# The same steps of an attention and gated feed-forward kernel in another hand-written order

## The chip, the core and the metric

The kernel runs on one core of one Trainium2 chip. A core has a matrix engine (TensorE, here PE, with its weight loads shown as PEld), a vector engine (DVE), a scalar engine (ACT), GpSimd (POOL) and a synchronization engine (SP). Each takes its own instructions in the order in which they are written, and waits for the others through semaphores. The time is that of one execution on the device in microseconds (us), a median over runs. TensorE writes into a small memory of eight banks, called bank 0 to 7 here; one bank holds 512 fp32 columns of 128 partitions.

## The reference

Eight batches, eight heads, 576 positions, head width 64. Linear attention without a softmax, a root-mean-square norm per head, then a gated feed-forward layer whose gate is a convolution over three positions:

```python
kv  = einsum('bhsd,bhse->bhde', k, v)
out = einsum('bhsd,bhde->bhse', q, kv)
rms = sqrt(mean(out * out, axis=-1, keepdims=True) + 1e-06)
x   = (out / rms * g_norm)              # heads side by side: (8, 576, 512)
h   = maximum(x @ w_in, 0.0)            # (8, 576, 1024)
conv_out = sum(conv_w[k] * hp[:, k:k + S, :] for k in range(3))   # hp: h padded by one row
gate = 1.0 / (1.0 + exp(-conv_out))
result = h * gate @ w_out               # (8, 576, 512)
```

## The kernel before

The whole program is a list of 697 short steps in one string, ORDER. A loop at the end takes one token after another and issues its instructions; then every instruction is tied to the one before it on its engine, so that each engine's order is exactly the string's. What stands between tokens of different engines plays no part: only the order on each engine, the data that a step reads, and the buffers that it reuses.

A token is a name with numbers, then an optional choice after a colon (which of ACT and DVE does a copy or a relu) and slots after an @ (which bank, or which buffer of a ring). `hm.2.4@0` is x @ w_in for batch 2 and the fifth of eight column blocks of 128, into banks 0 and 1. A step that writes into a bank waits until the steps that read the former contents are done. The choice differs by step: with `:1` a relu (re) goes to DVE, without it to ACT; kvn, ky, kvc, oc, ea and eh are the same; ca, qc0 and qc go to ACT with `:1` and to DVE without; dg goes to DVE with `:1`.

The steps, in the order in which a batch goes through them (line numbers are those of the kernel before):

- Loads, all from POOL's queue: `pre` (batch 0, in pieces of two heads, L245, and two more pieces from SP), Lq, Lk, Lv (one batch each, L304; batch 1 in two halves, `.0` and `.2`), Li.0 to Li.3 (w_in by quarters of its columns, L318; Li.1 holds column blocks 2 and 3), Lo.0 and Lo.1 (w_out by halves, L325). A load of a batch waits until its ring buffer (two for each of q, k and v) is free.
- kv: k^T v on PE (L361). Batches 0 and 1 copy it into a block-diagonal weight (kvc), the others into kvn, and with the halves of the partitions exchanged into kvx (ky, by an engine; kx, by SP's queue).
- q transposed: on PE (qt0, qt at L383; qtp at L391) and copied out (qc0, qc), or by SP's queue (dq, L439) for batches 5, 6 and 7.
- q (kv): ot on PE for batches 0 and 1 (L433, L434), oq for the others (L467), by tiles of two heads.
- The norm. Batches 0 and 1: sq (square, ACT, L494 or L496), on (sum over a head on PE), nl (reciprocal root, ACT, L545), mu0 (scale, DVE, L565); the last tile of batch 0 in halves: sqh (L517), onh (L523), nlh (L531), muh (L538). The others: sq and oc (square and plain copy, L496 and L344), ss (sums of all tiles on PE, L578), ln (root, L587), sl (split in two bf16 parts, DVE, L594 to L597), sp (spread over partitions on PE, L606), mu (L632); or fw, fr by way of memory for batches 6 and 7 (mu at L628). The root and the sigmoid of ACT need different tables; a table load (L217) is issued where ACT's order goes from one to the other, 12 times.
- hm: x @ w_in (L643), eight matmuls of 288 columns; ha and hb (L658, L666) are the same in two parts. re: the relu (L649 on ACT, L651 on DVE).
- The gate: ta (two taps, DVE, L702 and L703), aa and ab (adds, L709 and L715), sg (sigmoid, ACT, L748), mg (product, DVE, L754). Two column blocks of batch 0 take the three taps on PE instead (dg makes diagonal weights, L722; cm, L734; sg at L745).
- om: the product with w_out (L764) by tiles of 128 rows; for the first and last pair of batches in two parts (`.0` and `.4`); oh for the last tile (L781). ea, eh evict (L344 on ACT, L346 on DVE), st, sh store from SP's queue.
- `unread.n.i` issues n matmuls of ones that nobody reads (L430), 26 in all. pi, ps, pn, pg, pc, pl and ct make small constants: ct transposes the convolution's weights on PE, pc works out their ratios on DVE in six small instructions, ps and pl make the matrices that sp and ss use (pl by memsets on POOL).

The last lines of the program, which make the string the engines' order:

```python
    prev = {}
    for ins in list(nc.cur_bb.bb.instructions):
        e = ins.engine
        if e in prev:
            tc.add_manual_dep(
                ins, prev[e].name,
```

Of the kernel before, what the change touches and what calls it, by code (L numbers as in the profile page):

```python
# [850 lines left out]
```

## Time and profile before

| | |
|---|---|
| time, median of 3 runs | 176.29 us (176.2 to 176.9) |
| span of the profiled execution | 174.7 us |
| instructions profiled | 3978 |
| from HBM, to HBM | 34.88 MB, 9.73 MB |

The profiled execution has a span from its first to its last instruction of 174.7 us; the runs' times include 1.6 us more than that (176.29 - 174.7). A row of the timeline reads: start and length in us, engine, line, operation, what is written from what, how many were merged, and in brackets the idle time of the engine before it and what ended it. In the groups, the busy time and the mean length in ns stand behind the bar, then the idle time before. "q_sb" is the buffer of q, "bank" the matrix engine's banks, "xT" the normalized x, "h" the relu's result, "taps" the gate's buffers. "SPq" is SP's queue. For a DMA the time to landing runs from the start of its issue.

### The profile page before, as it was taken

What the parts mean: (1) busy time and instruction counts of PE and PEld (TensorE: products, weight loads), DVE (VectorE), ACT (ScalarE), POOL (GpSimd) and SP (SyncE); (2) the same over time, 40 slices, a digit from 0 to 9 for tenths busy, and PEclk for the clock granted to TensorE, in tenths of its full rate; (3) what the DMA queues carried; (4) which work ended last, traced back from release to release, by engine and by line L of the source; (5) the groups of instructions that cost most, each with busy time, mean ns of one, the idle gap of its engine ahead of it and who ended that gap; (6) DMA issues with size and microseconds to landing.
All of it is one profiled execution on the core that took longest, in us unless ns stands there. A gap on an engine that the chain in (4) does not pass through costs nothing.

```text
span 174.7 us, 3978 instructions
## 1 busy us (share of the span) xinstructions
PE 164.6 (94%) x1590; PEld 100.1 (57%) x1607; DVE 151.8 (87%) x248; ACT 144.0 (82%) x224; POOL 30.8 (18%) x54
## 2 busy tenths in 40 slices
PE   6988997899799999999999999999999999999992
PEld 2545765685644687744677774545687654444451
DVE  4166799999999999999999999999989999998520
ACT  4578897999999999999999998999988629766132
POOL 7994705313130001810000000000000000000000
PEclk9999999999999999999999999999999999999999
DMA  5999999999999999999999390477694400076285
GB/s 151 182 186 198 200 202 203 205 204 204 208 203 205 203 204 164 162 196 191 190 203 234 72 261 6 149 188 181 173 268 161 152 0 4 23 277 235 90 322 196
DMA packets 37450, 30.81 MB, mean 176 GB/s; under 512 B 8608, under 2 KB 32952, under 8 KB 37432
## 3 DMA queue, kind: packets, MB, share of 16 engines
q0 software_dynamic: 21760, 15.96, 60.7%
q1 hardware_dynamic: 15632, 14.59, 29.6%
q8 instruction: 12, 0.20, 0.4%
q14 instruction: 6, 0.05, 0.1%
q10 hardware_dynamic: 40, 0.01, 0.0%
HBM read 34.88 MB, written 9.73 MB: 255 GB/s over the span
## 4 chain that ended last, share of the span: by engine, by line
PE 76%; DVE 9%; DMA 4%; POOL 4%; ACT 2%; issue 2%; POOLq 0%; ACTq 0%
PE bank L764 35%; PE bank L643 30%; DMA w_in_sb<-in_moe_w_in_dram 4%; PE bank L361 3%; PE bank L467 2%; DVE taps L703 1%; DVE qT L346 1%; POOL q_sb L245 1%; DVE taps L709 1%; DVE h L754 1%; PE bank L606 1%; DVE taps L702 1%; POOL v_sb L245 1%; POOL k_sb L245 1%; PE bank L781 1%
## 5 line engine op out<-in xcount | busy, mean ns | idle before, releaser
L643 PE MATMUL bank<-xT,w_in_sb 128*128 128x288 bf16 x480 | 63.6, 286 | 0.3 <-ACT root L545 0.2
L764 PE MATMUL bank<-w_out_sb,h 128*128 128x512 bf16 x267 | 62.4, 379 | 0.8 <-issue 0.3
L643 PEld LDWEIGHTS <-w_in_sb 128*128 128x128 bf16 x480 | 46.0, 98 | 14.9 <-issue 1.6
L748 ACT ACTIVATE taps<-taps,cwn 128x1152 bf16<-128x1152 bf16 (+1 forms) x38 | 39.7, 1078 | 7.4 <-DVE taps L715 7.3
L764 PEld LDWEIGHTS <-h 128*128 128x128 bf16 x280 | 26.4, 98 | 31.0 <-issue 1.2
L649 ACT ACTIVATE h<-bank 128x576 bf16<-128x576 f32 x48 | 30.2, 656 | 3.0 <-PE bank L643 2.8
L344 ACT ACTIVATE row<-bank 128x512 f32<-128x512 f32 (+1 forms) x29 | 16.3, 595 | 8.8 <-PE bank L764 6.0
L754 DVE TENSOR_TENSOR h<-h,taps 128x2304 bf16<-128x2304 bf16 (+1 forms) x20 | 22.0, 1109 | 0.6 <-ACT taps L748 0.6
L709 DVE TENSOR_TENSOR taps<-taps 128x2304 bf16<-128x2304 bf16 (+1 forms) x19 | 21.5, 1134 | 0.2
L715 DVE TENSOR_TENSOR taps<-taps,h 128x2304 bf16<-128x2304 bf16 (+1 forms) x19 | 21.5, 1131 | 0.2
L496 ACT ACTIVATE sq<-bank 128x576 bf16<-128x576 f32 x28 | 17.8, 663 | 0.6 <-PE bank L467 0.3
L703 DVE TENSOR_SCALAR taps<-h,cwn 128x1152 bf16<-128x1152 bf16 (+1 forms) x38 | 17.8, 467 | 0.0
L702 DVE TENSOR_SCALAR taps<-h,cwn 128x1152 bf16<-128x1152 bf16 (+1 forms) x38 | 17.4, 457 | 0.3 <-ACT h L649 0.2
L217 ACT ACT_TABLE_LOAD x12 | 15.4, 1283 | 2.6 <-issue 2.4
L651 DVE TENSOR_SCALAR h<-bank 128x576 bf16<-128x576 f32 x16 | 11.8, 752 | 1.7 <-PE bank L643 0.8
L344 ACT ACTIVATE o<-bank 128x576 f32<-128x576 f32 x19 | 12.8, 674 | 0.0
L632 DVE SCALAR_TENSOR_TENSOR xT<-o,cw,bank 128x576 bf16<-128x576 f32 x16 | 12.2, 808 | 0.1
L304 POOL DMA_DIRECT2D q_sb<-in_q_dram x8 | 6.2, 770 | 30.2 <-PE bank L391 29.4
L430 PE MATMUL bank<-fill 128*128 128x512 bf16 x25 | 9.0, 481 | 1.5 <-DVE fill L232 1.5
L346 DVE COPY row<-bank 128x512 f32<-128x512 f32 (+1 forms) x8 | 5.4, 672 | 4.4 <-PE bank L781 2.4
L361 PE MATMUL bank<-v_sb,k_sb 96*64 96x64 bf16 x384 | 8.3, 197 | 0.7 <-ACT sq L496 0.5
L361 PEld LDWEIGHTS <-k_sb 96*64 96x64 bf16 x384 | 7.1, 112 | 2.9 <-issue 2.2
(94 smaller groups left out, 148.8 us busy)
## 6 DMA issues: line engine op xcount, KB each, us to landing
out_dram<-row SPq DMA_DIRECT2D x35, 256.0 KB, 2.6
q_sb<-in_q_dram POOLq DMA_DIRECT2D x6, 576.0 KB, 15.2
v_sb<-in_v_dram POOLq DMA_DIRECT2D x6, 576.0 KB, 14.6
k_sb<-in_k_dram POOLq DMA_DIRECT2D x6, 576.0 KB, 16.6
factor<-factor SPq DMA_DIRECT2D x8, 288.0 KB, 5.4
w_in_sb<-in_moe_w_in_dram POOLq DMA_DIRECT2D x4, 256.0 KB, 9.0
w_out_sb<-in_moe_w_out_dram POOLq DMA_DIRECT2D x2, 512.0 KB, 18.3
q_sb<-in_q_dram POOLq DMA_DIRECT2D x4, 144.0 KB, 4.7
```

Source lines behind the costliest of these rows:

```text
L344: nc.scalar.activation(to, fr, AX.Copy)
L361: nc.tensor.matmul(ps[i][i * D:(i + 1) * D, t - t0, :], k_sb[:, 2 * t + i, r * D:(r + 1) * D], v_sb[:, 2 * t + i, r * D:(r + 1) * D], star ...
L496: nc.scalar.activation(in_order(b, s), product(b, t), AX.Square)
L643: nc.tensor.matmul(ps[:, e, :HS], w_in_sb[:, t, f * P:(f + 1) * P], x[:, t, e * HS:(e + 1) * HS], start=(t == 0), stop=(t == NT - 1))
L649: nc.scalar.activation(to, fr, AX.Relu)
L702: nc.vector.tensor_scalar_mul(tap[:, 0, f % 2, :n, 8:8 + S], h[:, f], cwn[:, 0, f:f + 1])
L703: nc.vector.tensor_scalar_mul(tap[:, 1, f % 2, :n, :S], h[:, f], cwn[:, 2, f:f + 1])
L709: nc.vector.tensor_add(tap[:, 1, :, :n, :S], tap[:, 0, :, :n, 7:7 + S], tap[:, 1, :, :n, 1:1 + S])
L715: nc.vector.tensor_add(y, y, h[:, 2 * j:2 * j + 2])
L748: nc.scalar.activation(y, y, AX.Sigmoid, scale=cwn[:, 1, f:f + 1])
L754: nc.vector.tensor_mul(h, h, T["tap", c, j][:, 1, :, :n, :S])
L764: nc.tensor.matmul(T["om", p, m], h[:, f, m * P:(m + 1) * P], w_out_sb[:, f, :], start=(f == 0), stop=(f == NF - 1))
```

## The change

The string is replaced by another one. It has the same 697 steps with the same sizes; their order differs on all engines and in POOL's queue of loads, and so do the banks and ring buffers, and for 56 steps the choice between ACT and DVE. The beginning, before and after:

```diff
-pre@0,0,0 Lq.1.0@1 unread.10.0@1 qt0.0.0@0 qt0.0.1@1 ca.k.0:1 pi ca.v.0:1 qc0.0.0:1@0 unread.2.2@2
-kv.0.0.1@3 pn kv.0.1.1@2 kvc.0.0.1.0:1@0 kvc.0.0.1.1 kvc.0.1.1.1 qc0.0.1 unread.3.4@0 kvc.0.1.1.0 ot.0.1@4 ct@1
-unread.1.3@0 sq.0.1@0 pg Li.1 unread.2.1@2 on.0.1@0 ot.0.0@6 qt0.0.2@2 pc Li.3 nl.0.1@0 Lk.1.0@1 sq.0.0@0 al.x0@0
...
-Lq.1.2 ot.0.3@2 sqh.0.3.0@0 mu0.0.2 qt.1.0@0 sqh.0.3.1 onh.0.3.0@6 qc.1.0@0 onh.0.3.1 nlh.0.3.0@1 nlh.0.3.1 ha.0.2@4
-muh.0.3.1 ha.0.3@0 muh.0.3.0 ps dg.6 Lv.1.2 hm.0.6@6 dg.7 hb.0.2 re.0.2:1 hm.0.7@2 hb.0.3 re.0.6 cm.0.6@4 sg.0.6@0
+pre@0,0,0 Li.1 Lq.1.0@1 Li.3 al.x0@0 ca.k.0 Lk.1.0@1 unread.2.2@5 Lv.1.0@1 unread.10.0@0 ca.v.0 kv.0.0.1@5
+kvc.0.0.1.0@0 Li.0 Lk.1.2 al.h1@1 ps pi ct@7 pn qt0.0.1@0 pg dg.7:1 qt0.0.0@2 qc0.0.0:1@0 qc0.0.1 kv.0.1.1@7
...
+unread.2.1@3 ot.0.3@4 mu0.0.2 qt.1.0@2 qc.1.0@0 Lq.2.0@0 sqh.0.3.0@4 sqh.0.3.1 onh.0.3.0@0 onh.0.3.1 nlh.0.3.0@7
+muh.0.3.0 nlh.0.3.1 ha.0.2@6 ha.0.3@2 muh.0.3.1 hm.0.6@0 hb.0.2 pc hm.0.7@4 hb.0.3 Lv.2.0@0 al.h0@0 re.0.2:1 ta.0.2@0
```

Batch 1's norm, and the stretch up to the sums of batches 2 and 3:

```diff
-re.0.0:1 unread.3.1@0 ta.0.0@2 sq.1.0@0 on.1.0@2 nl.1.0@0 hm.0.1@0 ot.1.1@6 qt.1.1@2 re.0.1 ab.0.1 kv.1.2.2@0 mu0.1.0
-sq.1.1@0 kvc.1.2.2.1 on.1.1@4 qc.1.1@0 kvc.1.2.2.0 ot.1.3@2 mg.0.3 Li.2 ta.0.1 ot.1.2@0 nl.1.1@0 mu0.1.1 hm.0.4@4
...
-oq.2.3@0 Lk.3.0@1 aa.1.1 Lq.3.0@1 kv.3.0.4@4 ta.1.1 sq.2.2@2 sq.2.3@3 ss.2@5 kvn.3.0.4:1 re.1.4 oc.2.2:1@1 qtp.3.0@2
-Lo.0 oc.2.3 ky.3.0.4.1 ky.3.0.4.0 ln.8@0 qtp.3.1@0 qc.3.0@0 qc.3.1@1 oq.3.1@6 oq.3.0@2 ab.1.3 oq.3.2@0 sq.3.0@0
-oc.3.0@2 aa.1.0 sq.3.1@1 sl.8@0 om.0.1.0@4 Lo.1 oc.3.1 al.x2@0 ab.1.1 sq.3.2@2 om.0.3.0@5 om.0.2.0@2 Lq.4.0@0 oq.3.3@6
+ot.1.0@0 hm.0.0@2 re.0.0:1 hm.0.1@4 re.0.1:1 ta.0.0@2 sq.1.0@4 on.1.0@6 nl.1.0@4 mu0.1.0 ta.0.1 qt.1.1@2 qc.1.1:1@2
+ot.1.1@4 sq.1.1@4 unread.1.1@6 kv.1.2.2@7 kvc.1.2.2.1 Lk.3.0@1 kvc.1.2.2.0:1 Lv.3.0@1 aa.0.0 ab.0.0 on.1.1@0 nl.1.1@5
...
+kvn.3.0.4 hm.1.5@2 unread.3.1@7 oc.2.2@2 oc.2.3 qtp.3.0@0 re.1.5 ky.3.0.4.1:1 ss.2@4 ln.8@0 Lk.5.0@1 qtp.3.1@5
+Lq.5.0@1 qc.3.0@1 oq.3.0@0 sq.3.0@0 oq.3.1@2 sq.3.1@2 om.0.2.0@7 aa.1.0 om.0.3.0@4 oc.3.0@1 oc.3.1 ta.1.5 qc.3.1@1
+oq.3.2@5 sq.3.2@4 oc.3.2@3 om.0.1.0@0 oq.3.3@2 sq.3.3@3 oc.3.3 om.0.1.4 ea.0.1@1 om.0.3.4 ea.0.3@4 sl.8@0 sp.2.0@5,1
```

In that stretch qc.1.1, qc.2.1, kvn.2, kvn.3, oc.2.0 and oc.2.2 go from DVE to ACT, and re.0.1, re.1.2, re.1.6, kvc.1.2.2.0, ky.2.0.4.1 and both ky.3 from ACT to DVE. At the very beginning the casts ca and the diagonals dg go from ACT to DVE.

POOL's queue of loads: before Lq.1.0, Li.1, Li.3, Lk.1.0, Lv.1.0, Li.0, Lk.1.2, Lq.1.2, Lv.1.2, Li.2, Lq.2, pl, Lv.2, Lk.2, Lv.3, Lk.3, Lq.3, Lo.0, Lo.1, Lq.4, Lv.4, Lk.4, Lq.5, Lv.5, Lk.5, Lq.7, Lv.7, Lk.7, Lv.6, Lk.6, Lq.6; after Li.1, Lq.1.0, Li.3, Lk.1.0, Lv.1.0, Li.0, Lk.1.2, Lq.1.2, Lv.1.2, Li.2, Lk.2, Lq.2, Lv.2, Lk.3, Lv.3, Lq.3, Lo.0, Lo.1, Lq.4, Lk.4, pl, Lv.4, Lk.5, Lq.5, Lv.5, Lv.6, Lv.7, Lk.7, Lk.6, Lq.7, Lq.6.

The end:

```diff
-om.3.1.4 eh.3.8.0:1@4 st.2.5 ea.3.2@1 st.3.5 st.3.2 ea.3.3@2 st.3.3 om.3.7.4 ea.3.1@0 unread.1.2@0 sh.3.8.0 ea.3.7@0
-st.3.1 st.3.7 oh.3.8.1 eh.3.8.1 sh.3.8.1
+om.3.4.4 ea.3.4@1 st.3.4 st.3.3 om.3.7.4 ea.3.7@7 st.3.7 oh.3.8.0@1 eh.3.8.0@6 sh.3.8.0 oh.3.8.1 eh.3.8.1 sh.3.8.1
+unread.1.2@1
```

Because a ky may now stand ahead of its kvn, the two buffers of a batch are made before the loop:

```diff
+    for b in QUAD:
+        T["kvn", b] = consts.tile([P, NT, D], BF16, name=f"kvn{b}")
+        T["kvx", b] = consts.tile([P, NT, D], BF16, name=f"kvx{b}")
+
     @op
     def kvn(b, t0, n):
-        if t0 == 0:
-            T["kvn", b] = consts.tile([P, NT, D], BF16, name=f"kvn{b}")
-            T["kvx", b] = consts.tile([P, NT, D], BF16, name=f"kvx{b}")
         copy(T["kvn", b][:, t0:t0 + n], T["kvps", b, t0][0], pick[0] == 0)
```

83 lines of the change are left out of this document (42 added, 41 removed).

## The prediction

> **What bounds the kernel now.** I read the page first, then the busy times of five stretches, then the chain of waits from the end backwards, and last the single rows of the places that the change touches.
>
> ```profile
> span 174.7 us, 3978 instructions
> ...
> PE 164.6 (94%) x1590; PEld 100.1 (57%) x1607; DVE 151.8 (87%) x248; ACT 144.0 (82%) x224; POOL 30.8 (18%) x54
> ```
>
> The stretches (columns: stretch, its length, busy time of each engine, granted clock, share of the DMA engines, GB/s):
>
> ```profile
> 0.00:16.50 16.50, 13.96 (x157) 6.87 (x159) 7.88 (x30) 10.28 (x19) 13.09 (x24) 1.00 1.11 178
> 16.50:31.40 14.90, 13.28 (x157) 9.34 (x160) 13.10 (x25) 12.99 (x26) 7.62 (x18) 1.00 1.34 202
> 31.40:48.10 16.70, 15.04 (x252) 11.56 (x251) 16.44 (x35) 16.54 (x28) 3.84 (x6) 1.00 1.30 205
> 48.10:70.00 21.90, 21.79 (x223) 13.47 (x226) 21.59 (x38) 21.56 (x38) 2.28 (x4) 1.00 1.32 196
> 70.00:171.30 101.30, 100.52 (x805) 58.81 (x814) 92.80 (x123) 82.36 (x116) 4.01 (x5) 1.00 0.67 163
> ```
>
> From 48.1 us to the last matmul PE (first busy number) is idle for 0.11 + 0.78 = 0.89 us of 123.2. So the end is the moment at which PE gets through the door at 48 us, plus a dense run of work that the change leaves as it is. The door is set in the stretch before: from 31.4 to 48.1 us PE has 1.66 us of idle, while ACT (fourth number) has 0.16 and DVE (third) 0.26. There ACT and DVE are the bound together.
>
> The chain of waits (start, length, what) names what sets their start:
>
> ```profile
> 8.68 7.83 DMA w_in_sb<-in_moe_w_in_dram
> ...
> 16.55 1.65 PE bank L658 x12
> ...
> 31.59 1.54 DVE xT L565 x2
> ```
>
> A quarter of w_in, issued at 8.68 us, lets the first x @ w_in matmul (L658, ha.0.2) go at 16.55; then batch 1's normalization hands over to DVE at 31.59.
>
> **The change, part by part.** The same 697 steps are issued, so PE's work is the same; what counts is who waits. Where a copy or a relu changes between ACT and DVE, a few tenths are traded.
>
> *Loads in front.* The last load of batch 0 (v, issued 7.4), the first half of batch 1's q (8.0) and the w_in quarter (8.7), with their times from issue to landing:
>
> ```profile
> L245 POOL DMA_DIRECT2D v_sb<-in_v_dram x1: 629/629/629, 7.4 to 7.4; - x1
> ...
> DMA to landing us min/median/max: 5.8/5.8/5.8
> ```
>
> ```profile
> L304 POOL DMA_DIRECT2D q_sb<-in_q_dram x1: 691/691/691, 8.0 to 8.0; - x1
> ...
> DMA to landing us min/median/max: 6.6/6.6/6.6
> ```
>
> ```profile
> L318 POOL DMA_DIRECT2D w_in_sb<-in_moe_w_in_dram x1: 762/762/762, 8.7 to 8.7; - x1
> ...
> DMA to landing us min/median/max: 7.8/7.8/7.8
> ```
>
> They land at 13.2, 14.6 and 16.5: one after the other, and the next starts when the one before is through. With w_in first, it lands near 14.9 and the q half takes its place at 16.5 (16.1 if w_in needs only the 1.5 us of the q half). Gain: ha.0.2 waited 0.13 us for w_in, as these rows show (the matmuls in front of it, L523, end at 15.84 + 0.58 = 16.42):
>
> ```profile
> 15.21 0.70 PE L383 MATMUL bank<-ident,q_sb 96*64 96x96 bf16 x24
> 15.84 0.58 PE L523 MATMUL bank<-sq,ones 128*128 128x288 bf16 x2
> ```
>
> Price: the first row is qt.1.0, the transposes of that q half, at 15.21. The new PE order still has qt.1.0 in front of onh.0.3 (L523) and ha.0.2. So PE stands from 15.2 at the latest (its start in the row) to 16.5. Behind it queue both halves of onh, and with them ACT's last two roots of batch 0, DVE's muh, and all of x @ w_in. qt.1.0 at 16.5, onh 0.63 later, its two matmuls close together (their squares are long done) 0.25, so ha.0.2 at about 17.3: **+0.75 us** (0.4 if the half lands at 16.1). The rest of the prologue costs nothing: DVE is busy for 7.88 of its first 16.5 us, and takes the casts ca, the diagonals dg and ps into that idle time, where the ten plus two fills on PE cover them; pc, moved to behind muh, lies under the hm matmuls before the first relu. If that cover were gone, pc would delay the first relu by less than its own length, about a microsecond.
>
> By contrast the Trainium skill (DMA: Bandwidth & Descriptors, section "Anatomy of one DMA — SWDGE (gpsimd) path") fits a transfer by 2.0 us fixed plus its bytes at 436 GB/s; by that the two transfers behind v would move in an estimated 0.6 and 0.7 us and the wait would vanish. The trace does not agree: 3.3 us for the pair.
>
> *Batch 1's chain, 16.5 to 32.* Both orders run ACT square, PE sum, ACT root for four tiles. The new one lets three fills (unread.3.1) go elsewhere, but the root behind them waited for ACT's table load, not for PE. It takes a copy of 1152 columns (qc.1.1) onto ACT between the first root and the second square, and gives one relu and one small copy to DVE. With the costs below that is 1.0 - 0.53 - 0.14 = +0.3 on ACT; ACT has 1.9 us of idle in this stretch (14.90 - 12.99) to absorb a part. Followed by hand, the last root ends at about 32.85 instead of 32.19 (30.80 + 1.39, row below): **+0.65** so far (between +0.2 and +1.05).
>
> *ACT from 32 to 47.* The groups by form (busy, then mean ns of one):
>
> ```profile
> L649 ACT ACTIVATE h<-bank 128x576 bf16<-128x576 f32 x48 | 30.2, 656 | 3.0 <-PE bank L643 2.8
> ...
> L344 ACT ACTIVATE o<-bank 128x576 f32<-128x576 f32 x19 | 12.8, 674 | 0.0
> ...
> L344 ACT ACTIVATE kvx<-bank 64x256 bf16<-64x256 f32 x5 | 1.9, 378 | 0.1
> ...
> L344 ACT ACTIVATE kvn<-bank 128x256 bf16<-128x256 f32 x4 | 1.6, 389 | 0.0
> L344 ACT ACTIVATE qT<-bank 128x1152 bf16<-128x1152 bf16 x1 | 1.1, 1130 | 0.0
> ```
>
> ```profile
> 30.80 1.39 ACT L545 ACTIVATE root<-bank,eps_sb 128x576 f32<-128x576 f32 x2
> ...
> 46.98 1.28 ACT L217 ACT_TABLE_LOAD   x1
> 48.27 0.50 ACT L587 ACTIVATE rs<-bank,eps_sb 128x288 f32<-128x288 f32 x1
> 48.67 0.64 ACT L496 ACTIVATE sq<-bank 128x576 bf16<-128x576 f32 x1
> 49.20 0.65 ACT L344 ACTIVATE o<-bank 128x576 f32<-128x576 f32 x1
> 49.73 0.66 ACT L496 ACTIVATE sq<-bank 128x576 bf16<-128x576 f32 x1
> 50.26 0.67 ACT L344 ACTIVATE o<-bank 128x576 f32<-128x576 f32 x1
> ```
>
> The last four start 0.53 us apart though each takes 0.65: 0.13 overlaps. Between the last root and the table load for ln.8 ACT gains qc.2.1 (1.00), kvn.2 and kvn.3 (0.26 each) and oc.2.0 and oc.2.2 (0.54 each), and loses re.1.2 and re.1.6 (0.53 each) and three ky (0.38 each): 2.60 - 2.20 = +0.4; without overlap it would be +0.8. I take **+0.5**. DVE's counterpart comes out level with ACT: three relus and three ky in, four copies and two kvn out. So the table load for ln.8 goes from 46.98 to about 48.1, its root ends at 49.9, and the last copy above (oc.3.1, end 50.93) ends near 52.1.
>
> *The door.* The next row is PE's:
>
> ```profile
> 51.03 0.31 PE L467 MATMUL bank<-qT,kvn 64*64 64x288 bf16 x1
> ```
>
> This is oq.3.3, written into the banks that oc.3.1 has just emptied; the new order keeps that reuse (banks 2 and 3, from oq.3.1), and three half products om.0.x.0 stand in front of it in both orders. In the new order two of these wait as well: om.0.3.0 takes bank 4, which ln.8 reads, and om.0.1.0 takes bank 0, which oc.3.0 frees at about 51.55 in ACT's new sequence sq, sq, oc, oc. Then 0.86 for om.0.1.0, and oq.3.3 starts at about 52.45 instead of 51.03: **+1.4** (1.05 with oc.3.1 alone; 1.9 if ACT comes out at its far end). Behind oq.3.3 the same work remains for PE in either order.
>
> *The end.* A fill (unread.1.2) stands in front of the last product now, and behind it afterwards:
>
> ```profile
> 170.50 0.38 PE L430 MATMUL bank<-fill 128*128 128x512 bf16 x1
> ...
> 170.72 0.61 PE L781 MATMUL bank<-w_out_sb,h 128*128 128x128 bf16 x8
> ```
>
> That gives back the 0.22 between them. Of the 0.89 us of idle in the dense run I let 0.2 go, as waits of before are met by work from another place (bounds 0 and 0.45). The other reordering, of stores, of sel's memsets on POOL and of relus behind 70 us, I cost at nothing: there ACT has 18.9 and DVE 8.5 us of idle to hide it.
>
> **Sum**, against the profiled execution: 174.7 + 1.4 - 0.22 - 0.2 = 175.7 us of span. The median 176.29 lies 1.6 above that span, so **177.3 us**, +0.6%; from its bounds 176.6 to 178.3.
>
> **Rivals.**
>
> *The shift is absorbed.* ACT's 1.9 us of idle between 16.5 and 31.4 takes up the late start, and only its added 0.5 arrives at the door: 176.29 + 0.5 - 0.22 - 0.2 = 176.4. For it speaks that idle; against it that each ACT step there waits for PE or DVE steps which start 0.75 late too.
>
> *Faster: the loads aren't served one by one.* If the q half is moved beside w_in and lands by 15.2, nothing waits: ha.0.2 gains 0.13, the three fills leave batch 1's stretch (3 x 0.22 = 0.65), ACT's added 0.4 remains: -0.4 at the door. With 0.22 at the end and half of the 0.89, 175.2. It decides at a landing of the q half before 15.2. Against it stand the landings above; by the skill's fit it would be the likely one.
>
> *Slower still: batch 7's queries come late.* Lq.7.0 was the first of the six last loads, and becomes the fifth, behind Lv.6, Lv.7, Lk.7 and Lk.6. Rows: its landing, the transposing DMAs' (SP queue), and the first oq of batch 7.
>
> ```profile
> L304 POOL DMA_DIRECT2D q_sb<-in_q_dram x1: 769/769/769, 69.1 to 69.1; - x1
> ...
> DMA to landing us min/median/max: 8.0/8.0/8.0
> ```
>
> ```profile
> L439 SPq DMA_TRANSPOSE qT<-q_sb x6: 1326/1833/4900, 61.9 to 99.4; - x6
> ...
> DMA to landing us min/median/max: 3.7/6.9/11.6
> ```
>
> ```profile
> 95.15 0.31 PE L467 MATMUL bank<-qT,kvn 64*64 64x288 bf16 x1
> ```
>
> It landed at 77.1, 18 us ahead of use. As the fifth, with four loads of 2.9 us (twice the 1.45 of a half) in front, it lands near 89. A transposing DMA of 3.7 to 6.9 us is then through by 93 to 96, and PE, 1.4 late, wants it near 96.6: just in time. At the far end (11.6) PE waits 4 us. With 1.5 us as what lies between: 178.8. It decides when dq.7.0 lands after oq.7.0's turn.
>
> **How the numbers follow.** I give the forecast 0.50, absorbed 0.11, faster 0.14, late queries 0.25. What a measurement of this kernel can tell from no change is about 0.5%, 0.88 us: above 177.17 is slower, below 175.41 faster. The forecast's 0.50 falls 0.33 above that line and 0.17 below. Slower 0.33 + 0.25 = 0.58, same 0.17 + 0.11 = 0.28, faster 0.14. The range runs from the faster case, 175.2, to 179.3, 0.5 above the latest; the forecast's own is 176.6 to 178.3.
>
> **What would show it.** Right: qt.1.0 starts on PE at 16.2 to 16.6 with a wait for q_sb's DMA before it, and ha.0.2 at 17.0 to 17.5; the table load before ln.8 at 47.8 to 48.5; PE idle before om.0.1.0 or oq.3.3 for bank readers on ACT; oq.3.3 at 52 to 53; PE dense from there. Wrong: a q half that lands before 15.5; a dense PE run that begins before 48; or a PE wait of over 0.5 us behind 70 us, above all at an oq of batches 5 to 7.

## The result and the profile after

The changed kernel takes **186.12 us** (median of 4, 185.38 to 188.37) against 176.29 us: 1.053 times as long (95% interval 1.049 to 1.057). The forecast was 177.3, with a range up to 179.3. The profiled execution has a span of 184.6 us and took 186.38. Here and below a median is over all runs of a kernel, while its ratio leaves out runs that are more than 1.5% above the fastest one.

From the page of the changed kernel:

```profile
span 184.6 us, 4002 instructions
...
PE 169.6 (92%) x1607; PEld 101.0 (55%) x1607; DVE 155.8 (84%) x258; ACT 143.1 (78%) x214; POOL 30.4 (16%) x54
```

The stretches of the changed kernel, in the columns of the prediction (after the first two come PE, PEld, DVE, ACT, POOL, then the granted clock); the first four are those of before:

```profile
0.00:16.50 16.50, 12.97 (x131) 6.13 (x131) 9.10 (x34) 6.47 (x12) 13.47 (x25) 0.90 1.12 178
16.50:31.40 14.90, 13.82 (x182) 9.66 (x181) 13.66 (x30) 11.75 (x20) 5.59 (x8) 1.00 1.34 202
31.40:48.10 16.70, 14.81 (x216) 10.74 (x216) 16.40 (x35) 15.31 (x25) 5.09 (x15) 1.00 1.30 205
48.10:70.00 21.90, 20.18 (x227) 11.45 (x225) 19.82 (x35) 20.57 (x34) 2.46 (x3) 1.00 1.29 205
70.00:130.00 60.00, 60.00 (x588) 36.17 (x587) 58.65 (x82) 58.03 (x86) 3.82 (x5) 1.00 0.79 151
130.00:137.50 7.50, 3.76 (x31) 2.86 (x30) 6.77 (x10) 2.96 (x6) 0.00 (x0) 1.00 0.65 178
137.50:142.20 4.70, 4.68 (x25) 3.18 (x25) 3.61 (x4) 3.45 (x4) 0.00 (x0) 0.64 0.89 335
```

Three places differ: a granted clock of 0.90 in front, PE's idle time between 48 and 55 us (the door), and 3.74 us of idle PE at 130 to 137.5, called the hole below, with a clock of 0.64 behind it. From 70 to 130 us PE is never idle.

**In front.** PE's timeline (start, length, what; in brackets the idle time ahead of it and who ended it), then two windows:

```profile
8.79 0.38 PE L361 MATMUL bank<-v_sb,k_sb 96*64 96x64 bf16 x12 [1.07 <-DMA v_sb<-in_v_dram]
9.11 1.46 PE L430 MATMUL bank<-fill 128*128 128x512 bf16 x3
...
16.80 0.70 PE L383 MATMUL bank<-ident,q_sb 96*64 96x96 bf16 x24
```

```profile
5.70:9.10 3.40, 2.05 (x52) 1.34 (x50) 2.82 (x14) 0.87 (x2) 3.26 (x6) 0.99 1.28 183
9.10:12.40 3.30, 3.30 (x15) 1.30 (x11) 1.25 (x6) 1.19 (x2) 3.11 (x5) 0.50 1.27 184
```

PE waits 1.07 us for the second v load in front of kv.0.1.1 (the row at 8.79), and for the next 3.3 us the clock is 0.50: three fills take 1.46 us, where before three took 0.81 or 0.82. Little of this wait is due to the order: both strings have twelve fills ahead of kv.0.1.1, and PE is through with what precedes it at 8.79 - 1.07 = 7.72, before at 7.91. The load landed late, 5.0 us after its issue at 3.66, where in the profile of the kernel before it took 4.2. qt.1.0 comes at 16.80 instead of 15.21, with no wait for its q half, which landed at 8.95 + 7.0 = 15.95 us (issue and landing of its one DMA).

**The door.** Timelines of DVE, ACT and PE:

```profile
47.23 0.56 DVE L703 TENSOR_SCALAR taps<-h,cwn 128x576 bf16<-128x576 bf16 x1
47.71 0.35 DVE L704 TENSOR_SCALAR taps<-h,cwn 128x576 bf16<-128x576 bf16 x1
48.09 0.42 DVE L346 CAST kvx<-bank 64x256 bf16<-64x256 f32 x1
48.97 0.42 DVE L346 CAST kvx<-bank 64x256 bf16<-64x256 f32 x1 [0.45 <-ACT kvn L344]
```

```profile
48.55 0.39 ACT L344 ACTIVATE kvn<-bank 128x256 bf16<-128x256 f32 x1 [1.33 <-DVE kvx L346]
48.83 1.19 ACT L344 ACTIVATE o<-bank 128x576 f32<-128x576 f32 x2
...
50.58 1.28 ACT L217 ACT_TABLE_LOAD   x1
```

```profile
32.95 2.23 PE L644 MATMUL bank<-xT,w_in_sb 128*128 128x288 bf16 x16 [0.29 <-ACT root L546]
...
49.53 0.67 PE L391 MATMUL bank<-ident,q_sb 96*128 96x96 bf16 x12 [1.20 <-ACT o L344]
...
54.05 1.02 PE L765 MATMUL bank<-w_out_sb,h 128*128 128x512 bf16 x4 [0.35 <-ACT o L344]
55.01 0.31 PE L468 MATMUL bank<-qT,kvn 64*64 64x288 bf16 x1
```

Three copies read one kv bank (ky, kvn, ky) and follow each other across the engines. The first is now on DVE, behind six tap instructions (ta.1.0, ta.1.1 and ta.1.4; the last two are shown); ACT stands 1.33 us for it, behind ACT's kvn the two oc copies (L344, o) wait, behind them PE's qtp.3.0 (L391, 49.53). From hm.0.5 (32.95; before: next row) to oq.3.3 (55.01) PE takes 22.06 us, before 51.03 - 31.61 = 19.42: **+2.64**, on top of +1.34 in front.

```profile
31.61 1.14 PE L643 MATMUL bank<-xT,w_in_sb 128*128 128x288 bf16 x8 [0.22 <-ACT root L545]
```

**The hole.** The chain of waits of the changed kernel (start, length, what), ACT's timeline, the SP queue's, PE's, and three windows:

```profile
128.17 1.47 ACT row L344 x3
...
129.94 6.30 DMA out_dram<-row
...
136.33 0.60 ACT row L344
136.93 0.55 ACT h L650
```

```profile
136.33 0.60 ACT L344 ACTIVATE row<-bank 128x512 f32<-128x512 f32 x1 [3.84 <-DMA out_dram<-row]
```

```profile
126.63 2.57 SPq L621 DMA_DIRECT2D factor<-factor  x4
129.30 1.05 SPq L801 DMA_DIRECT2D out_dram<-row  x2
```

```profile
137.52 10.65 PE L644 MATMUL bank<-xT,w_in_sb 128*128 128x288 bf16 x72 [3.76 <-ACT h L650]
```

```profile
135.34:138.75 3.41, 1.23 (x11) 0.98 (x11) 3.38 (x4) 2.42 (x4) 0.00 (x0) 1.00 0.30 109
138.75:142.16 3.41, 3.41 (x17) 2.16 (x15) 2.40 (x3) 2.20 (x3) 0.00 (x0) 0.50 0.94 355
142.17:145.58 3.41, 3.41 (x30) 2.72 (x29) 1.56 (x4) 2.60 (x4) 0.00 (x0) 1.00 0.00 0
```

In the new order ea.1.6, the next row copy after ea.1.0, gets the same row buffer 0, which st.1.0 is to empty first. That store stands on SP behind four broadcasts of 288 KB for batch 7 (L621) and lands 6.3 us after its issue. ACT waits 3.84 us for it at the head of its queue, re.6.6 (L650) behind it, and PE for re.6.6's bank. 1.2 us after PE goes on, the clock halves for 3.41 us.

### The profile page after: what moved, and what is told of

It reads as the page before. It is cut to its first block, busy times and chain, and to the rows that moved or that the text cites. A ratio compares the mean times of both kernels' runs of the same rounds, so it can differ in the third digit from the quotient of the medians.

```text
span 184.6 us, 4002 instructions
## 1 busy us (share of the span) xinstructions
PE 169.6 (92%) x1607; PEld 101.0 (55%) x1607; DVE 155.8 (84%) x258; ACT 143.1 (78%) x214; POOL 30.4 (16%) x54
## 4 chain that ended last, share of the span: by engine, by line
PE 55%; DVE 21%; ACT 11%; DMA 6%; issue 3%; POOL 1%; SPq 0%; POOLq 0%; ACTq 0%; DVEq 0%
PE bank L644 23%; PE bank L765 22%; DMA out_dram<-row 3%; DVE h L652 3%; ACT L217 3%; DMA v_sb<-in_v_dram 3%; DVE taps L703 3%; ACT taps L749 3%; DVE taps L716 2%; DVE taps L704 2%; DVE taps L710 2%; PE bank L361 2%; DVE xT L566 2%; ACT row L344 2%; PE bank L430 2%
## 5 line engine op out<-in xcount | busy, mean ns | idle before, releaser
L644 PE MATMUL bank<-xT,w_in_sb 128*128 128x288 bf16 x480 | 65.6, 291 | 4.4 <-ACT h L650 4.0
L765 PE MATMUL bank<-w_out_sb,h 128*128 128x512 bf16 x280 | 64.2, 379 | 0.4 <-ACT o L344 0.4
L644 PEld LDWEIGHTS <-w_in_sb 128*128 128x128 bf16 x480 | 46.8, 99 | 20.5 <-issue 5.7
L650 ACT ACTIVATE h<-bank 128x576 bf16<-128x576 f32 x48 | 30.5, 655 | 6.4 <-PE bank L644 5.9
L344 ACT ACTIVATE row<-bank 128x512 f32<-128x512 f32 (+2 forms) x31 | 17.9, 588 | 17.0 <-PE bank L765 12.4
L703 DVE TENSOR_SCALAR taps<-h,cwn 128x1152 bf16<-128x1152 bf16 (+1 forms) x38 | 18.2, 479 | 3.1 <-ACT h L650 2.8
L704 DVE TENSOR_SCALAR taps<-h,cwn 128x1152 bf16<-128x1152 bf16 (+1 forms) x38 | 17.9, 472 | 0.0
L344 ACT ACTIVATE o<-bank 128x576 f32<-128x576 f32 x20 | 12.7, 672 | 0.0
L430 PE MATMUL bank<-fill 128*128 128x512 bf16 x26 | 10.2, 527 | 1.6 <-DVE fill L232 1.5
L304 POOL DMA_DIRECT2D v_sb<-in_v_dram x8 | 6.0, 748 | 24.3 <-PE bank L607 11.5
L304 POOL DMA_DIRECT2D k_sb<-in_k_dram x8 | 6.0, 753 | 12.9 <-PE bank L361 11.5
```

Source lines behind the costliest of these rows:

```text
L344: nc.scalar.activation(to, fr, AX.Copy)
L644: nc.tensor.matmul(ps[:, e, :HS], w_in_sb[:, t, f * P:(f + 1) * P], x[:, t, e * HS:(e + 1) * HS], start=(t == 0), stop=(t == NT - 1))
L650: nc.scalar.activation(to, fr, AX.Relu)
L703: nc.vector.tensor_scalar_mul(tap[:, 0, f % 2, :n, 8:8 + S], h[:, f], cwn[:, 0, f:f + 1])
L704: nc.vector.tensor_scalar_mul(tap[:, 1, f % 2, :n, :S], h[:, f], cwn[:, 2, f:f + 1])
L765: nc.tensor.matmul(T["om", p, m], h[:, f, m * P:(m + 1) * P], w_out_sb[:, f, :], start=(f == 0), stop=(f == NF - 1))
```

## The experiments

Times in us; the starts are those of the profiled execution; "door" is hm.0.5 to oq.3.3, "rest" oq.3.3 to the start of the last product, oh.3.8.1. The ratio is to the kernel before, measured together with it (95% interval).

| kernel | time | ratio | ha.0.2 | hm.0.5 | door | rest |
|---|---|---|---|---|---|---|
| before | 176.29 | | 16.55 | 31.61 | 19.42 | 119.69 |
| changed | 186.12 | 1.053 (1.049 to 1.057) | 17.90 | 32.95 | 22.06 | 125.61 |
| e1_row | 181.64 | 1.029 (1.023 to 1.034) | 17.52 | 32.57 | 22.04 | 120.24 |
| e2_warm | 185.34 | 1.054 (1.049 to 1.059) | 16.72 | 31.77 | 22.05 | 125.13 |
| e3_ky | 185.01 | 1.039 (1.033 to 1.045) | 16.48 | 31.54 | 21.45 | 123.10 |
| e4_loads | 177.04 | 1.006 (1.003 to 1.009) | 16.93 | 31.36 | 19.43 | 119.92 |
| e5_fr | 189.11 | 1.063 (1.057 to 1.069) | 17.32 | 32.56 | 22.04 | 126.41 |
| e6_picks | 190.68 | 1.069 (1.062 to 1.077) | 16.82 | 35.38 | 25.71 | 123.25 |
| e7_stallfill | 184.17 | 1.044 (1.041 to 1.048) | 17.99 | 33.30 | 22.04 | 123.68 |
| e8_end | 176.40 | 1.000 (0.998 to 1.003) | 16.56 | 30.99 | 19.42 | 120.21 |
| e9_ta | 185.88 | none | 17.63 | 32.86 | 20.74 | 126.95 |
| e10_kyqc | 185.96 | 1.045 (1.040 to 1.051) | 18.46 | 35.18 | 21.03 | 125.58 |
| e11_three | 180.31 | 1.023 (1.019 to 1.027) | 17.06 | 32.12 | 22.05 | 121.34 |
| e12_all | 179.16 | 1.015 (1.011 to 1.019) | 16.64 | 31.69 | 20.65 | 120.70 |
| e13_qc | 179.27 | 1.013 (1.006 to 1.021) | 16.56 | 31.61 | 21.31 | 120.42 |
| e14_qcoc | 180.31 | 1.020 (1.012 to 1.028) | 16.18 | 31.58 | 22.02 | 120.88 |
| e15_qcky | 178.57 | 1.010 (1.002 to 1.018) | 16.84 | 31.91 | 20.28 | 120.42 |

The kernels that keep the hole scatter by several us from run to run, since a half-rate spell, 3.4 us long, is there in one run and not in the next (the changed kernel's mean clock is 0.982 in two runs and 0.991 in two; a spell is 3.41 x 0.5 / 184.6 = 0.009); for these the stretches say more than the medians. The four times of e9_ta (182.35 to 186.32) give no ratio. The late hm.0.5 of two profiles has half-rate spells ahead of it: in e10_kyqc from 18.86 to 22.26 us, in e6_picks from 28.82 to 39.05.

### The hole at 132 us

**e1_row**: another buffer.

```diff
-re.6.4 ea.1.6@0 st.1.6
+re.6.4 ea.1.6@8 st.1.6
```

> The changed kernel, but the row copy ea.1.6 writes into a ninth row buffer, so that it no longer waits for the store st.1.0. Theory: the ACT wait of 3.84 us at 132.5 and the 3.3 us of half TensorE clock behind it (138.8 to 142.1) belong together; lateness against before stood at 5.69 us ahead of the wait and at 10.2 behind it, so both go: 186.1 - 4.5 = 181.6 us, no ACT wait for out_dram<-row over 0.5 us, granted clock 1.00 from 130 to 150. Rival: the next row buffers wait for stores too (the same SP queue), the wait moves by a step and under 2.5 us come back: 183.6 or more.

The median is the theory's 181.6, though that is partly luck: the four runs lie between 180.15 and 184.53, and this profile also kept its clock in front. The stretch is firmer: the rest falls from 125.61 to 120.24. PE's timeline of this kernel runs through, without a wait and at a clock of 1.00:

```profile
128.47 13.80 PE L644 MATMUL bank<-xT,w_in_sb 128*128 128x288 bf16 x111
```

**5.4 us** of the rest hang on this one buffer. The other 0.55 by which the rest exceeds that of before (120.24 - 119.69) stay open.

**e7_stallfill**: the wait stays, PE is kept busy.

```diff
-ta.3.6@0 ta.3.7 hm.6.0@6
+ta.3.6@0 ta.3.7 unread.16.9@0 hm.6.0@6
```

> The changed kernel with sixteen fill matmuls (3.5 us) on PE in front of hm.6.0, where PE stands idle for 3.8 us; the ACT wait for the store stays. Theory: the idle time is what drops the clock to half for 3.3 us afterwards; with PE busy the clock stays 1.00 from 130 to 150, hm.6.0 still waits as long, but from hm.6.0 to hm.7.7 PE takes 7.8 us (as in the run with the ninth row buffer) instead of 9.5, and the time is 1.6 below: 184.5. Rival: the drop has another cause (the store traffic, heat): 9.5 us again, 186.

184.17, near the theory's 184.5. PE's timeline of this kernel:

```profile
134.14 3.62 PE L430 MATMUL bank<-fill 128*128 128x512 bf16 x16
137.59 8.98 PE L644 MATMUL bank<-xT,w_in_sb 128*128 128x288 bf16 x72
```

hm.6.0 starts as late as ever (137.59), but 72 matmuls take 8.98 us instead of 10.65: about 1.7 us, half of a spell of 3.41, and the rest is 1.9 shorter. So of the 5.4 us some 3.5 to 3.7 are the wait and the others the clock.

**e5_fr**: the broadcasts go behind the two stores.

```diff
-fr.7.1@0 fr.7.0@1
...
-ea.1.0@0 st.1.0 al.h3@1
+ea.1.0@0 st.1.0 fr.7.1@0 fr.7.0@1 al.h3@1
```

> The changed kernel, but on SP the four broadcasts fr.7.1 and fr.7.0 (288 KB each) go behind the stores st.1.8 and st.1.0 instead of ahead of them; the row buffers stay as they are. Theory: the store st.1.0 is late because these transfers stand in front of it; alone it lands about 2.6 us after its issue near 128.6, so ea.1.6 on ACT waits under 0.5 us and the time is near that of the ninth row buffer, 181 to 182; the broadcasts land near 136, before mu.7 wants them at 139. Rival: seven copies are too short a distance for a row buffer whatever stands in front: ACT still waits 2 us or more for out_dram<-row and the time is 184 or more.

Half right, and no faster: 189.11. (The distance is one row copy, not seven: ea.1.6 is the next one after ea.1.0.) The stores st.1.8 and st.1.0 now land 2.0 us after their issue, and ACT no longer waits for them (hm.6.0 starts at 133.44), so the transfers in front were what delayed st.1.0. But mu.7 on DVE now waits for the broadcasts. DVE's timeline of this kernel:

```profile
135.60 1.55 DVE L629 SCALAR_TENSOR_TENSOR xT<-o,cw,factor 128x576 bf16<-128x576 f32 x2 [3.31 <-DMA factor<-factor]
138.97 1.55 DVE L629 SCALAR_TENSOR_TENSOR xT<-o,cw,factor 128x576 bf16<-128x576 f32 x2 [1.82 <-DMA factor<-factor]
```

PE then stands 4.28 us for mu.7's x. One queue serves two waiting engines: here reordering it moved the wait, and a buffer removed it.

### The front

**e2_warm**: fills over the gap.

```diff
-qc0.0.1 kv.0.1.1@7
+qc0.0.1 unread.5.9@4 kv.0.1.1@7
```

> The changed kernel with five more fill matmuls on PE in front of kv.0.1.1, where PE waits 1.07 us for v_sb's load. Theory: this gap is what lets the clock fall to half from 9.1 to 12.4 us; with it filled the clock stays 1.00, on.0.1 starts near 11.5 instead of 12.54, ha.0.2 near 17.0 instead of 17.90, and some 0.9 us come through to the end: 185.2. Rival: batch 0 is late for its order (casts on DVE behind the second v load), not for the clock: on.0.1 gains under 0.3 us and the end is 185.9 to 186.3. A second rival: ha.0.2 is early by 0.9 but the door at 48 us takes it back: oq.3.3 stays at 55.0 and the time at 186.

The same two windows of this kernel:

```profile
5.70:9.10 3.40, 3.40 (x57) 1.79 (x55) 2.80 (x14) 0.87 (x2) 3.40 (x6) 1.00 1.25 188
9.10:12.40 3.30, 3.04 (x46) 1.58 (x38) 1.72 (x8) 2.17 (x5) 3.07 (x5) 1.00 1.31 189
```

Clock 1.00, on.0.1 at 10.94 instead of 12.54, ha.0.2 at 16.72, and 1.2 us come through to the door (oq.3.3 at 53.82 instead of 55.01). In the time it can't be told from the scatter: e1_row, with its clock at 1.00 too, has ha.0.2 at 17.52, since its q half lands later (row below). The fills suffice (in the 24 runs of e11 to e15, which all have them and lack the hole, the mean clock is 0.997 or more), but not every run needs them: e1_row, without them, waited only 0.73 us at this place and kept its clock. In it appears what the half clock had hidden in the changed kernel:

```profile
16.63 0.70 PE L383 MATMUL bank<-ident,q_sb 96*64 96x96 bf16 x24 [1.17 <-DMA q_sb<-in_q_dram]
```

That is the predicted wait of qt.1.0 for its q half. The profiles of seven kernels with both the new string's order of loads and a full clock up to there show it, between 0.57 us (e2_warm) and 2.52 us (e10_kyqc); their ha.0.2 starts between 16.48 and 18.46, in the median at 17.32.

**e4_loads**: the kernel before with this order of loads alone.

```diff
-pre@0,0,0 Lq.1.0@1
+pre@0,0,0 Li.1 Lq.1.0@1
...
-pg Li.1 unread.2.1@2
+pg unread.2.1@2
```

> The kernel before with one part of the change alone: the w_in quarter Li.1 issued ahead of the q half Lq.1.0. Theory of the prediction: the q half lands near 16 instead of 14.6, qt.1.0 on PE waits for it from 15.2 to 16, ha.0.2 starts 0.7 us late and the door and the end with it: 177.0. Rival: the slack between 16.5 and 31.4 takes it up: ha.0.2 late by 0.7, the end within 0.2 of 176.3.

The median, 177.04, is the theory's 177.0, and the interval of the ratio (1.003 to 1.009) lies above 1. The profiled execution, with 176.49 among the shortest of twelve, shows the rival: qt.1.0 at 15.88 (+0.67), ha.0.2 at 16.93 (+0.38), and by on.1.1 nothing is left of it (27.51, before 27.72). But its 0.67 are not the predicted wait. PE was late by them since kv.0.1.1, which waited for the v load (4.9 us to landing), as PE's timeline of this kernel shows:

```profile
8.61 0.38 PE L361 MATMUL bank<-v_sb,k_sb 96*64 96x64 bf16 x12 [0.76 <-DMA v_sb<-in_v_dram]
```

The q half landed at 8.9 + 6.9 = 15.8, just ahead of the late qt.1.0. So this profile shows a q half that comes late for a PE on time (15.8 against 15.21), but not the wait itself.

### The door

**e9_ta**: one copy on DVE ahead of three steps.

```diff
-re.1.0 ta.1.0@2 ta.1.1 hm.1.4@2 re.1.4 ta.1.4@1 oq.2.3@4
+re.1.0 hm.1.4@2 re.1.4 oq.2.3@4
...
-kvn.3.0.4 hm.1.5@2
+kvn.3.0.4 ta.1.0@2 ta.1.1 ta.1.4@1 hm.1.5@2
```

> The changed kernel with DVE's copy ky.3.0.4.0 ahead of the three steps ta.1.0, ta.1.1 and ta.1.4 instead of behind them; every copy stays on its engine. Theory: what stands in front of this copy on DVE makes kvn.3 on ACT late, and through oc.2.2 PE's qtp.3.0: kvn.3 starts 1.3 us earlier and from hm.0.5 to oq.3.3 PE needs 20.8 to 21.2 us instead of 22.06, and the time is 1 us below the changed kernel's. Rival: ACT and DVE have the same work to do in this stretch in any order, and qc.3.0 on DVE now waits for the ta steps: 21.8 or more.

Timelines of ACT and of PE in this kernel:

```profile
47.06 0.38 ACT L344 ACTIVATE kvn<-bank 128x256 bf16<-128x256 f32 x1
```

```profile
48.06 0.68 PE L391 MATMUL bank<-ident,q_sb 96*128 96x96 bf16 x12
...
53.60 0.31 PE L468 MATMUL bank<-qT,kvn 64*64 64x288 bf16 x1
```

The door takes 20.74 us: **1.3 of the 2.64** were the three steps in front of one copy. The gain didn't reach the end in the profiled execution, where a second row buffer became a wait (e11_three).

**e3_ky**: the three ky on ACT.

```diff
-ky.2.0.4.1:1
+ky.2.0.4.1
...
-ky.3.0.4.0:1
+ky.3.0.4.0
...
-ky.3.0.4.1:1
+ky.3.0.4.1
```

> The changed kernel with the three small copies ky.2.0.4.1, ky.3.0.4.0 and ky.3.0.4.1 back on ACT, as before. Theory: on DVE they stand behind three pairs of taps, and kvn.3, which reads the same PSUM bank on ACT, waits 1.33 us for them with two oc copies queued behind it, which PE's qtp.3.0 waits for. On ACT: kvn.3 ends near 47.8 instead of 48.94, qtp.3.0 starts near 48.5 instead of 49.53, oq.3.3 near 54 instead of 55.01, end 185.1. Rival: DVE is the bound of the stretch anyway, or ACT pays with 1.1 us more work what it no longer waits: qtp.3.0 moves, oq.3.3 stays within 0.3 of 55.0, end 185.8 to 186.3.

Between the two: qtp.3.0 1.0 us nearer to hm.0.5, but the door only 0.6 shorter (21.45). ACT pays 1.1 us of copies for the waits it saves.

**e6_picks**: twelve copies and relus back on their engines of before.

```diff
-re.0.1:1
+re.0.1
...
-qc.1.1:1@2
+qc.1.1@2
...
-kvc.1.2.2.0:1
+kvc.1.2.2.0
...
-re.1.2:1
+re.1.2
...
-qc.2.1:1@1
+qc.2.1@1
...
-kvn.2.0.4
+kvn.2.0.4:1
...
-oc.2.0@0
+oc.2.0:1@0
...
-re.1.6:1
+re.1.6
...
-kvn.3.0.4
+kvn.3.0.4:1
...
-oc.2.2@2
+oc.2.2:1@2
```

with the three ky of e3_ky.

> The changed kernel with the engine of twelve copies and relus of batches 0 to 3 (23 to 52 us: re.0.1, qc.1.1, kvc.1.2.2.0, re.1.2, qc.2.1, three ky, kvn.2, kvn.3, oc.2.0, oc.2.2, re.1.6) set back to that of before; the order stays. From hm.0.5 to oq.3.3 PE needs 19.42 us before, 22.06 in the changed kernel, 21.45 with the three ky alone on ACT. Theory: the engine of these copies makes the door late: 19.4 to 20.2, and the time 2 us below the changed kernel's, 184. Rival: the order on the engines does (qtp.3.0 and ln.8 behind oc.2.3, the relus behind three pairs of taps): 21 us or more, time 185.3 or more.

25.71 us, and hm.0.5 itself 2.4 later than in the changed kernel; but this profile ran at half clock from 28.82 to 39.05 us and from 56.13 to 59.53, as two windows show:

```profile
28.82:39.05 10.23, 9.36 (x59) 5.07 (x59) 8.23 (x16) 7.76 (x13) 3.80 (x5) 0.50 1.31 203
56.13:59.53 3.40, 3.40 (x15) 1.09 (x16) 3.29 (x8) 2.28 (x4) 1.61 (x2) 0.50 1.31 204
```

Some 7.1 us of the door (39.05 - 35.38 and 3.4) were at half clock, which can have cost at most half of that. An estimate without it is 25.71 - 3.5 = 22.2 us, no better than the changed kernel's 22.05 and far from the theory's 20.2. So the rival stands: the choice of engine alone isn't what makes the door late, as far as one disturbed profile can show.

**e10_kyqc, e13_qc, e14_qcoc, e15_qcky** ask what the other 1.2 us are. e10 is e3_ky with qc.2.1 on DVE; e13 and e14 are e12_all (below) with qc.2.1, and with qc.2.1 and oc.2.2, on DVE; e15 is e13 with ky.2.0.4.1 on ACT.

```diff
-qc.2.1:1@1
+qc.2.1@1
...
-oc.2.2@2
+oc.2.2:1@2
...
-ky.2.0.4.1:1
+ky.2.0.4.1
```

> The changed kernel with the three ky on ACT and the copy qc.2.1 (1.11 us on ACT, 0.75 on DVE) back on DVE. With the ky alone ACT was busy without a break from 40 to 54 us and DVE idle for 1.6 us. Theory: ACT's work is then the bound of the door: without qc.2.1 on it PE needs 20.3 to 20.8 us from hm.0.5 to oq.3.3 (21.45 with the ky alone). Rival: the gain is stopped by qtp.3.0's bank, which oc.2.2 frees after two squares, whatever ACT did before: 21.2 or more.

> As the kernel with all found causes undone, and qc.2.1 back on DVE (0.67 us of DVE's time for 1.0 us of ACT's). From hm.0.5 to oq.3.3 PE took 20.65 us there, with ACT busy without a break from 42.6 us to the end of the stretch. Theory: ACT's extra copies are what is left of the door's lateness: 19.8 to 20.2 us, time 0.5 to 0.8 below that kernel's. Rival: DVE, which has only 0.9 us of idle time in the stretch, takes it back: 20.5 or more and the time unchanged.

> As e13_qc, and oc.2.2 on DVE as well (0.66 us for 0.53 us). Theory that ACT is the bound: another 0.3 to 0.5 us off the stretch from hm.0.5 to oq.3.3, 19.4 to 19.8. Rival: DVE is level with ACT by now and delays ky.3.0.4.1 and qc.3.0: no better than e13_qc, or 0.3 worse.

> As e13_qc, and batch 2's small copy ky.2.0.4.1 on ACT. In e13_qc ACT waited 1.5 us for this copy, which stood on DVE behind qc.2.1 and the steps after it. Theory: the rest of the door's lateness is this second hand-off between DVE and ACT in one PSUM bank; with ky.2.0.4.1 on ACT and qc.2.1 on DVE ACT has 0.6 us less to do than with all causes undone and waits for nothing: 19.8 to 20.2 us from hm.0.5 to oq.3.3. Rival: the two engines are level and the order of their steps is the rest: 20.5 or more.

e10: 21.03, between theory and rival. e13: 21.31, worse than e12's 20.65 (its time the same within the intervals), because the next hand-off between the engines grew, from 0.5 us in e12 to 1.5. ACT's waits in e13_qc (total, times, longest):

```profile
ACT kvx L344 <- DVE kvx L346: 1.5, 1, 1.5
```

e14: 22.02, worse again. e15, without that hand-off: 20.28. So neither ACT's nor DVE's load alone is the rest; in e13 and e14 what one engine saved was paid on the other. The last 0.9 us (20.28 - 19.42) stay open; no run undid the order of the steps itself.

### The end, and all together

**e8_end**: the kernel before with the fill behind the last product.

```diff
-ea.3.1@0 unread.1.2@0 sh.3.8.0
+ea.3.1@0 sh.3.8.0
...
-oh.3.8.1 eh.3.8.1 sh.3.8.1
+oh.3.8.1 eh.3.8.1 sh.3.8.1 unread.1.2@1
```

> The kernel before with one part of the change alone: the fill unread.1.2 stands behind the last product instead of ahead of it. Prediction's term: the last product om.3.7.4 to oh.3.8.1 is 0.22 us closer, the end 0.22 earlier: 176.0. Rival: PE waits there for a row or bank reader anyway, and the end stays within 0.05.

From oh.3.8.0 to oh.3.8.1 PE takes 170.62 - 167.59 = 3.03 us instead of 170.72 - 167.47 = 3.25: the 0.22 are there, but the time can't show them.

**e11_three**: the edits of e1_row and e2_warm, and the q half first.

```diff
-pre@0,0,0 Li.1 Lq.1.0@1 Li.3
+pre@0,0,0 Lq.1.0@1 Li.1 Li.3
```

> The changed kernel with three of its parts undone: a ninth row buffer for ea.1.6, five fills in front of kv.0.1.1, and the q half Lq.1.0 ahead of Li.1 as before. Theory (all lateness is in four places: front, door 2.64, behind the door 0.55, stall with its clock 5.4): what is left is the door and the 0.55, less what the end gains: 176.3 + 2.6 + 0.5 = 179.4 (179 to 180), ha.0.2 within 0.2 of 16.55, no half clock. Rival: with the front on time another wait there or behind 110 us comes up, and the time is 180.5 or more.

180.31, between the two: qt.1.0 at 15.39 without a wait, no half clock, but a new wait behind the door. ACT's timeline of this kernel, and the one store issued from 79 to 85 us:

```profile
88.39 0.60 ACT L344 ACTIVATE row<-bank 128x512 f32<-128x512 f32 x1 [1.35 <-PE bank L644]
```

```profile
L801 SPq DMA_DIRECT2D out_dram<-row x1: 368/368/368, 81.1 to 81.1; - x1
...
DMA to landing us min/median/max: 7.2/7.2/7.2
```

ea.0.5 takes row buffer 5 two row copies after ea.0.8 had it, and st.0.8 lands at 81.1 + 7.2 = 88.3. The bracket names PE's bank; by the times it was the store. In the changed kernel everything is late enough for it not to show.

**e12_all**: as e11_three, with a free buffer for ea.0.5, the order of e9_ta on DVE, and ta.1.4 and ta.1.5 still later.

```diff
-om.0.5.4 ea.0.5@5
+om.0.5.4 ea.0.5@3
...
-oc.3.1 ta.1.5 qc.3.1@1
+oc.3.1 qc.3.1@1
...
-sl.8@0 sp.2.0@5,1
+sl.8@0 ta.1.4@1 ta.1.5 sp.2.0@5,1
```

> The changed kernel with all found causes undone at once: ninth row buffer for ea.1.6, buffer 3 instead of 5 for ea.0.5 (it waited up to 1.35 us for the store st.0.8), the five fills, the q half in front again, and on DVE ky.3.0.4.0 ahead of ta.1.0 and ta.1.1, with ta.1.4 and ta.1.5 behind sl.8 (before had them behind the door too). Theory: the door's lateness is what DVE does ahead of it, namely the taps brought forward: PE needs 19.9 to 20.4 us from hm.0.5 to oq.3.3 (20.74 with ky moved alone, 19.42 before), and the time is 176.3 + 0.7 + 0.5 = 177.5 (176.9 to 178.2). Rival: ACT, with 1.5 us more copies than before, is the bound there: 20.6 or more, and the time 178.2 or more.

179.16, and the door 20.65: the rival's numbers. Moving two more taps gained nothing over e9_ta. No version of the new order beats the one before; e15_qcky comes nearest, 1.0% behind (0.2 to 1.8).

## Why the prediction was wrong

The direction was right, the size not: +1.0 us forecast, +9.8 measured. Profile against profile, the start of oh.3.8.1 is 9.90 us later: 1.34 in front, 2.64 at the door, 5.92 behind it, of which 5.37 are the hole (125.61 - 120.24).

*The step that failed* first of all is "The other reordering, of stores, of sel's memsets on POOL and of relus behind 70 us, I cost at nothing: there ACT has 18.9 and DVE 8.5 us of idle to hide it." Idle time in total hides nothing from a wait at the head of an in-order queue. The diff shows row buffer 0 reused by the very next row copy, with four broadcasts ahead of the store in SP's queue; the queues were to be followed there as they were in front. e1_row shows its price: with its clock it is 5.4 us, more than half of the whole loss, and alone it would take the time past 179.3 (176.29 + 5.4 = 181.7). But without it e1_row still takes 181.64, so the door, the second term that failed, leads out of the range too. Of the signs of being wrong one did come, the PE wait of over 0.5 us behind 70 us, though not at an oq: 3.76 us at hm.6.0.

*Loads in front*: right mechanism, about the right size, and hidden in the changed kernel's own profile. The q half landed at 15.95 (16.1 to 16.5 predicted), and qt.1.0 waits for it in all seven profiles of the new string that keep the clock up to there. Their ha.0.2, 17.32 in the median, fits "about 17.3", but with a scatter of 2 us a single profile could have missed it (the prediction's own terms, 16.5 + 0.63 + 0.25, add up to 17.38). The load order by itself costs 0.6% (0.3 to 0.9) in e4_loads, though its profile doesn't show where. "The rest of the prologue costs nothing" left out the loads of batch 0: where the second v load lands late, PE stands at kv.0.1.1, and in the changed kernel the half clock follows and ha.0.2 starts at 17.90.

*Batch 1's chain*: +1.34 at hm.0.5 against +0.65; it hands on what it gets (+1.35 at ha.0.2): from ha.0.2 to hm.0.5 the profiles of the changed kernel, e1_row, e2_warm and e3_ky all take 15.05 or 15.06 us, before 15.06. That ACT's idle time absorbs a late start holds in the order of before (in e4_loads' profile), not in the new one.

*ACT 32 to 47 and the door*: +0.75 predicted beyond the late start (1.4 - 0.65), +2.64 measured; the table load before ln.8 starts at 50.58, where 47.8 to 48.5 was predicted. The reuse of banks 0, 2 and 3 is as described; PE does wait 0.35 us for oc.3.0 in front of om.0.1.0 (54.05). But "DVE's counterpart comes out level with ACT" counts only work. It missed what stands in front of a copy on DVE that ACT waits for: 1.3 us (e9_ta). Without that, the door is 1.2 to 1.3 late, against 0.75.

*The end*: 0.22 between the last products in e8_end's profile, as predicted. (The upper end of the forecast's own range, 178.3, doesn't follow from its bounds: 174.7 + 1.9 - 0.22 + 1.6 = 178.0. This changes nothing here.)

*Rivals*: batch 7's queries came in time (PE without idle time from 70 to 130 us); "absorbed" and "faster" did not happen. None of the rivals had a store in it, though the price of this kind, late by a queue, was worked out for the loads.

## What to carry to other kernels

When an order changes, check for every buffer that is reused how many steps lie between its store and its next writer, and what stands in front of that store in its DMA queue; an extra buffer removed such a wait here, and a new order of the queue only moved it. Where copies of one bank are split over two engines, the later one inherits the whole queue of the other: cost the position, not the work. And a gap on PE can cost more than its length, a spell at half clock behind it: keep fills ahead of a wait, not behind it.

## What the hardware showed

The half-rate spells last 3.41 us or a multiple of it (10.23 in e6_picks), and the clock changes only at fixed places in a profile: in the changed kernel at 9.04, 12.45, 138.75 and 142.16 us, and 138.75 - 12.45 = 126.30 us are 37 stretches of 3.41 (3.4135) us. So what counts is how busy PE was between two such places, and not the length of a gap alone. In e2_warm the hole is 3.04 us of idle PE, nearly all in one such stretch; in e3_ky it is 2.92 us, spread over two, and the clock stays. (Where the clock never changes, as in e3_ky and e1_row, the stretches are counted from the start of the trace's record of the clock, 7.36 and 4.70 us.) Windows of e2_warm, then of e3_ky:

```profile
132.44:135.85 3.41, 0.40 (x4) 0.19 (x2) 2.76 (x4) 1.16 (x3) 0.00 (x0) 1.00 0.34 124
135.86:139.26 3.40, 3.38 (x15) 2.08 (x15) 3.37 (x4) 2.79 (x3) 0.00 (x0) 0.50 0.94 350
```

```profile
130.24:133.65 3.41, 1.49 (x13) 1.06 (x11) 2.77 (x5) 0.40 (x2) 0.00 (x0) 1.00 0.70 207
133.65:137.06 3.41, 2.40 (x20) 1.93 (x20) 3.38 (x4) 3.41 (x5) 0.00 (x0) 1.00 0.64 237
137.07:140.48 3.41, 3.41 (x30) 2.72 (x29) 2.47 (x5) 2.82 (x6) 0.00 (x0) 1.00 0.59 223
```

At the hole the clock fell behind stretches with PE busy for 0.40 and 1.23 us (the changed kernel) and not behind 1.49. In front it fell behind 2.05 of 3.40 us, and in e1_row, whose stretch runs from 4.71 to 8.11, not behind 2.28. So there is no one limit for all kinds of matmuls. The Trainium skill (TensorE: Matmul & The Clock Gate, section "What's actually happening") has a free-running window of 3413 ns, and half rate after at least one idle window of about 3.4 us. The length of the spells and their fixed places agree; that a window must be idle doesn't, in front least of all, and by that rule the front would have cost only its wait.

A store of 256 KB lands 2.3 us after its issue in the median of the changed kernel's 35. It took 6.3 us behind the broadcasts, and 5.8 to 7.2 us for st.0.8 in four kernels (the changed one, e1_row, e9_ta, e11_three), which is what made the distance of one and of two row copies too short.
